# Three local changes and new step durations in a planner that orders a fused attention and expert kernel

## The chip, the core and the metric

The kernel runs on one core of a Trainium2 chip. The core has a matrix engine (PE, with its weight loads as PEld), a vector engine (DVE), an activation engine (ACT), a general engine (POOL) and a queue that issues transfers (SP). The metric is the device time of one execution in microseconds; lower is better. Matrix products write to PSUM, which has eight banks here, each of 128 x 512 float32.

## The reference, cut to what matters

```python
# stage 1: batch 4, 8 heads, 576 positions, 64 per head; heads 0-3 local (32 back), 4-7 strided (every 32nd)
scores = where(mask, q @ k.T / 8, -1e9); a = exp(scores - max)
attn = a / (a.sum(-1) + 1e-9) @ v
# stage 2: x (4, 576, 512)
h = relu(x @ w_in); u, v = h[..., :512], h[..., 512:]
v_n = (v - mean(v)) / sqrt(var(v) + 1e-6)
g = u * (w_spatial @ v_n + b_spatial);  x = g @ w_out
# stage 3: four experts, two of them chosen for each position by a gate
a_e = causal softmax((x wq_e) (x wk_e).T / 8), again with + 1e-9 in the divisor
out = sum over chosen e of weight_e * (a_e @ (x wv_e)) @ wo_e
```

All is float32; a product is made of three products of high and low parts.

## The kernel before, in words

Every piece of work is a *step* of a Python generator. A step says on which engine it runs (or on which of several), how long it is expected to take, what it waits for, and which buffers and PSUM banks it takes. A planner (`Plan.run`) plays the steps against these durations, takes on each engine the step that can start first (the lower rank among those that start within 0.05 us of it), and so fixes the order of the instructions on each engine. The chip runs each engine's list in that order, and semaphores keep the data right. A duration or a rank therefore changes no work, but the order, and with a choice of engines also the engine.

PSUM banks are shared out by kind: `d` for dense products (4), `s` for scores (2), `t` for transposes (2), `x` for values (3), eight of them at any time. `a1_scores` takes both `s` banks at once, `a1_values` two `x` banks.

Stage 1 for one pair of heads goes so: load q, k, v (SP); scores (PE, L497 or L507); mask and row maximum (DVE, L520 local, L555 strided); exponentials with row sums (ACT, L526, L561); `over_sums`, which adds 1e-9 to the sums (DVE, L534), inverts them (DVE, L535) and multiplies the rows (L537, DVE or POOL by the planner's choice); transposes (PE, L582) and values (PE, L640); high and low parts `xh`, `xl` (ACT and DVE, L652). There are four pairs per batch.

The first products with `w_in` need its words turned from float64 into float32 parts (`weight`: DVE L344 to L349). For the four blocks of the v half the sum of the two parts runs through PE (`summed`: L357 to L359 into an `s` bank, then a copy). The u half uses L371 (add) and L378 (low part) instead.

`v_half` makes the v half (PE, L289 to L291, 128 x 512), then `normalize`: statistics (DVE, L711 to L715), a power on POOL (`rstd`, L717), the scaling (DVE, L719), and the parts `vh` (ACT) and `vlo` (L699, mostly POOL). `u_half` is L289 to L291 with 128 x 288. `spatial` (PE, L794 to L799) needs all five v tiles of a batch. `late_constants` fills masks and zero tiles for stage 3 on POOL (L264 to L277): `mqk`, `mtail`, `bd`, `alone`, `tri`.

Where the planner sees PE without work in the first 46 us, it puts in products of zeros (`fill`, L217), one for each 0.4268 us that it expects to be free.

Of the kernel before, what the change touches and what calls it, by code (L numbers as in the profile page):

```python
# [7 lines left out]
F = dt.float32  # L8
R = dt.float32r
I32 = dt.int32  # L10
AF = mybir.ActivationFunctionType
# [142 lines left out]
def fused(tc, qk, vl, vs, win, wsb, woutT, wp, wo, out):  # L154
# [168 lines left out]
    def weight(keys, src, r0, rows, c0, cols, after=(), summed=False, alone=False):  # L323
# [10 lines left out]
        else:  # L334
# [6 lines left out]

            yield "dve", t_fast(2 * cols, 2) + t_dve(cols) + 0.25, (), dict(c=2)
            a, p2 = C([rows, cols], I32, "a"), C([rows, cols], I32, "p2")
# [7 lines left out]
            if summed:  # L351
                yield *hi_of(cols), (), dict(c=1)
                hi = C([rows, cols], R, "wh")
                copy(hi, f(a))
                yield "pe", t_mm(cols, 6), (), dict(s=1)
                ps = P([rows, cols], "s")
                pe.matmul(ps, ident, f(a), start=True, stop=False)  # L357
                pe.matmul(ps, unit, m, start=False, stop=False)
                pe.matmul(ps, minus, hi, start=False, stop=True)  # L359
                plan.give("c", 3)  # L360
                yield *out_of(cols), (), dict(c=1)
                wl = C([rows, cols], R, "wl")
                copy(wl, ps)
                plan.give("s")
                key, = keys
                W[key] = (hi, wl)
                plan.set(("W", key))
                return
# [111 lines left out]
    def a1_scores(b, hp):  # L480
# [4 lines left out]
        n = [len(a1_blocks(hp, g)) for g in range(2)]  # L485
        yield "pe", sum(n) * (0.1 if local else 0.09), [("qk", b, hp)], dict(s=2)
        st = A1[b, hp]
# [23 lines left out]
    def a1_local(b, hp, g):  # L511
        c0, c1 = LOCAL_GROUPS[g]
        n = c1 - c0
        yield "dve", t_dve(n * 64, n), [("mask", True), ("s1", b, hp)], dict(c=1)
        st = A1[b, hp]

        mx = sm([128, 8], "mx")
        a = C([128, n, 64], F, "a")
        for c in range(n):
            dve.tensor_tensor_reduce(a[:, c], st["ps"][g][:, c], mloc[:, min(c0 + c, 1)], op0=ALU.add, op1=ALU.min,  # L520
                                     scale=-0.125, scalar=3.0e38, accum_out=mx[:, c:c + 1])
        plan.give("s")
        yield "act", t_act(n * 64, n, 0.27), (), {}
        sums = sm([128, 8], "sums")
        for c in range(n):
            act.activation(a[:, c], a[:, c], AF.Exp, bias=mx[:, c:c + 1], scale=-1.0, accum_out=sums[:, c:c + 1])  # L526
        yield from over_sums(a, sums)
        st["a"][g] = a
        plan.set(("a", b, hp, g))

    def over_sums(x, sums):
        _, n, nk = x.shape
        yield "dve", 0.3, (), {}
        dve.scalar_tensor_tensor(sums[:, :n], sums[:, :n], 1e-9, sums[:, :n], op0=ALU.add, op1=ALU.max)  # L534
        dve.reciprocal(sums[:, :n], sums[:, :n])  # L535
        yield ("dve", "pool"), (t_dve(n * nk), t_pool(n * nk)), (), {}
        engine().tensor_mul(x, x, sums[:, :n].unsqueeze(2).broadcast_to([128, n, nk]))  # L537

    def a1_strided(b, hp, g):
# [17 lines left out]
        plan.give("s")  # L557
        yield "act", t_act(n * 54, n, 0.23), (), {}
        sums = sm([128, 8], "sums")
        for j, w in enumerate(width):  # L560
            act.activation(a[:, j, :w], a[:, j, :w], AF.Exp, bias=mx[:, j:j + 1], scale=-1.0,  # L561
                           accum_out=sums[:, j:j + 1])
        yield from over_sums(a[:, :n, :54], sums)
# [32 lines left out]
    def a1_values(b, hp):  # L596

        local = hp < 2
        yield ("pe", 18 * 0.05 if local else 11 * 0.07, [("v1", b, hp)] + [("aT", b, hp, g) for g in range(2)],
               dict(x=2))  # L600
# [41 lines left out]
        for g, part in enumerate(runs):  # L642
            cn = 64 * ((NL + 1 - g) // 2) if local else 54 * (4, 6)[g] + 36 * g
            yield *out_of(cn, len(part)), (), {} if g else dict(c=2)
            if g == 0:
                st["x"] = (C([128, S], R, "xh"), C([128, S], R, "xl"))
            xh, xl = st["x"]
            for cols, src in part:
                copy(cols(xh), src)
            yield "dve", t_dve(cn, len(part)), (), {}  # L650
            for cols, src in part:
                dve.tensor_sub(cols(xl), src, cols(f(xh)))  # L652
            if local:
                plan.give("x")
            elif g:
                plan.give("x", 2)
            plan.set(("x", b, hp, g))
# [46 lines left out]
    def normalize(ps, result):  # L704
# [12 lines left out]
        pool.tensor_tensor(rstd, rstd, neghalf, op=ALU.pow)  # L717
        yield "dve", t_fast(512, 1, 0.19), (), {}
        dve.tensor_scalar(vr, vr, mv[:, 0:1], rstd, op0=ALU.subtract, op1=ALU.mult)  # L719
# [386 lines left out]
    def a2_values(b, e):  # L1106
# [27 lines left out]
        copy(hi, px[:64])  # L1134
        yield "dve", t_dve(1024, 2), (), {}
        dve.tensor_sub(lo, px[:64], f(hi))
# [4 lines left out]
    def a2_tail_values(b, p):  # L1141
# [23 lines left out]
        for o in range(2):  # L1165
            copy(hi[o], px[:64, o, 0])
        yield "dve", t_dve(64, 6), (), {}
        for o in range(2):
# [51 lines left out]

    plan.add(90, late_constants())

# [135 lines left out]
```

## Time and profile before

| | us |
|---|---|
| median of three timed runs | 442.07 |
| the three runs | 441.53, 444.05, 442.07 |
| span of the profiled execution | 440.9 |
| PE busy in it | 424.2 |
| DVE busy | 312.2 |
| ACT busy | 282.2 |
| POOL busy | 140.0 |

The profiled execution shows its span and no other time; the median stands 1.2 us above that span. PE's clock was granted in full in every stretch up to the last one (1.00; 0.96 from 430 us on), the upper of its two levels, 2.4 GHz.

### The profile page before, as it was taken

Reading aid. Unit: us, or ns where it says so; the run is one execution under the profiler, and the core shown is the slowest. Engines: PE = TensorE matmul, PEld = TensorE weight load, DVE = VectorE, ACT = ScalarE, POOL = GpSimd, SP = SyncE. Lnnn points to the kernel's source line nnn. Section 1 sums busy time; section 2 is a strip of 40 time slices with the busy share of each in tenths; the row PEclk is TensorE's granted clock in tenths of the full one; section 3 lists DMA queues with packets and bytes.
Section 4 is the critical chain, followed back from the end, with each engine's and each line's share of the span. In section 5 each row is a group of like instructions: output and inputs, shape, how many; then the busy total and the mean of one; then the engine's idle time right before and its main releaser. Section 6 shows DMA issues by size and latency. Waiting matters only on the chain.

```text
span 440.9 us, 12067 instructions
## 1 busy us (share of the span) xinstructions
PE 424.2 (96%) x4424; PEld 382.0 (87%) x4429; DVE 312.2 (71%) x1155; ACT 282.2 (64%) x927; POOL 140.0 (32%) x237
## 2 busy tenths in 40 slices
PE   7798889999999999999999999999999999999996
PEld 4576679898999889998998899999999899988884
DVE  5879988545722783327998646789888998987861
ACT  4688598427930886205633533987787799769972
POOL 3317897422400371002675900021211111112300
PEclk9999999999999999999999999999999999999999
DMA  8998109200483005001000043711540415061234
GB/s 270 361 362 281 39 2 315 82 1 4 115 287 139 4 2 170 24 1 43 7 1 0 1 112 82 161 42 30 124 112 4 105 40 121 1 155 73 96 97 143
DMA packets 22814, 44.20 MB, mean 100 GB/s; under 512 B 3170, under 2 KB 5218, under 8 KB 22756
## 3 DMA queue, kind: packets, MB, share of 16 engines
q1 hardware_dynamic: 22756, 43.44, 33.2%
q8 instruction: 35, 0.57, 0.6%
q14 instruction: 23, 0.19, 0.1%
HBM read 27.18 MB, written 4.72 MB: 72 GB/s over the span
## 4 chain that ended last, share of the span: by engine, by line
PE 77%; DVE 11%; ACT 6%; POOL 2%; issue 2%; DVEq 0%; POOLq 0%; ACTq 0%
PE pd L289 14%; PE pd L291 14%; PE pd L290 14%; PE pd L794 4%; PE pd L795 4%; PE pd L796 4%; PE pt L1074 3%; PE px L640 3%; PE px L1120 2%; PE px L1122 2%; PE ps L497 2%; PE pt L582 2%; PE ps L990 2%; PE ps L989 2%; ACT a L1008 1%
## 5 line engine op out<-in xcount | busy, mean ns | idle before, releaser
L1001 ACT ACTIVATE a<-a,amx 128x128 f32<-128x128 f32 (+1 forms) x64 | 35.5, 556 | 6.7 <-DVE amx L977 6.3
L289 PE MATMUL pd<-xh,wh 128*128 128x288 f32 x128 | 39.0, 305 | 0.3 <-DVE mx L555 0.3
L289 PE MATMUL pd<-gh,fh 128*128 128x288 f32 x128 | 38.1, 298 | 0.0
L291 PE MATMUL pd<-gh,fl 128*128 128x288 f32 x128 | 37.9, 296 | 0.2 <-DVE fl L436 0.2
L794 PE MATMUL pd<-wh,vh 128*128 128x288 f32 x128 | 37.8, 295 | 0.0
L526 ACT ACTIVATE a<-a,mx 128x64 f32<-128x64 f32 x72 | 23.9, 334 | 21.5 <-DVE mx L520 21.5
L796 PE MATMUL pd<-wh,vlo 128*128 128x288 f32 x128 | 37.7, 294 | 0.0
L291 PE MATMUL pd<-xh,wl 128*128 128x288 f32 x128 | 37.7, 294 | 0.0
L290 PE MATMUL pd<-xl,wh 128*128 128x288 f32 x128 | 37.7, 294 | 0.0
L795 PE MATMUL pd<-wl,vh 128*128 128x288 f32 x128 | 37.7, 294 | 0.0
L290 PE MATMUL pd<-gl,fh 128*128 128x288 f32 x128 | 37.7, 294 | 0.0
L802 DVE TENSOR_TENSOR u<-pd,u 128x288 f32<-128x288 f32 x32 | 14.3, 453 | 31.7 <-PE pd L799 31.6
L977 DVE CUSTOM_DVE_ANT_0 a<-ps,mqk 128x128 f32<-128x128 f32 (+4 forms) x72 | 32.5, 481 | 4.3 <-PE ps L990 2.9
L537 POOL TENSOR_TENSOR a<-a,sums 128x320 f32<-128x320 f32 (+3 forms) x31 | 22.8, 736 | 38.1 <-DVE sums L535 17.4
L1008 ACT ACTIVATE a<-a,asums 128x384 f32<-128x384 f32 (+3 forms) x52 | 28.7, 566 | 6.6 <-DVE asums L1018 6.5
L561 ACT ACTIVATE a<-a,mx 128x54 f32<-128x54 f32 (+1 forms) x88 | 28.5, 335 | 3.2 <-DVE mx L555 3.2
L1010 POOL TENSOR_SCALAR a<-a,asums 128x256 f32<-128x256 f32 (+3 forms) x12 | 11.7, 977 | 59.1 <-DVE asums L1018 39.9
L1063 DVE TENSOR_TENSOR e<-pt,e 128x384 fp32r<-128x384 f32 (+1 forms) x48 | 27.5, 598 | 2.8 <-ACT e L310 2.3
L652 DVE TENSOR_TENSOR xl<-px,xh 128x108 fp32r<-128x108 f32 (+4 forms) x48 | 19.2, 433 | 14.4 <-ACT xh L310 14.4
L289 PE MATMUL pd<-wh,xh 128*128 128x512 f32 x64 | 26.5, 414 | 0.0
L316 ACT ACTIVATE vr<-pd 128x512 f32<-128x512 f32 x16 | 9.4, 593 | 25.8 <-PE pd L291 25.6
L1074 PE MATMUL pt<-ident,a 128*128 128x128 f32 x160 | 24.3, 275 | 1.0 <-ACT a L1008 1.0
(228 smaller groups left out, 1481.8 us busy)
## 6 DMA issues: line engine op xcount, KB each, us to landing
qk<-qk SPq DMA_DIRECT2D x64, 144.0 KB, 2.6
q<-in_qk_dram SPq DMA_DIRECT2D x16, 288.0 KB, 4.5
k<-in_qk_dram SPq DMA_DIRECT2D x16, 288.0 KB, 4.7
w<-in_win_dram SPq DMA_DIRECT2D x8, 512.0 KB, 6.1
v<-in_vl_dram SPq DMA_DIRECT2D x16, 256.0 KB, 5.4
out_dram<-o SPq DMA_DIRECT2D x16, 256.0 KB, 2.0
v<-in_vs_dram SPq DMA_DIRECT2D x8, 256.0 KB, 4.9
w<-in_woutT_dram SPq DMA_DIRECT2D x4, 512.0 KB, 6.3
```

The costliest lines, as they stand in the source:

```text
L289: pe.matmul(ps, ah, bh, start=i == 0, stop=False)
L290: pe.matmul(ps, ah, bl, start=False, stop=False)
L291: pe.matmul(ps, al, bh, start=False, stop=i == n - 1)
L561: act.activation(a[:, j, :w], a[:, j, :w], AF.Exp, bias=mx[:, j:j + 1], scale=-1.0, accum_out=sums[:, j:j + 1])
L794: pe.matmul(ps, vh[:, fs], wh[:, c0:c0 + cn], start=(i == 0), stop=False)
L795: pe.matmul(ps, vh[:, fs], wl[:, c0:c0 + cn], start=False, stop=False)
L796: pe.matmul(ps, vlo[:, fs], wh[:, c0:c0 + cn], start=False, stop=False)
L977: dve.tensor_tensor_reduce(a[:, s0:s0 + sn], ps, mask, op0=ALU.add, op1=ALU.min, scale=-0.125, scalar=m if s0 else 3.0e38, accum_out=m)
L1001: act.activation(a, a, AF.Exp, bias=m, scale=-1.0, accum_out=st["sums", e][:, i:i + 1])
L1008: act.activation(a, a, AF.Copy, scale=r)
L1063: dve.tensor_sub(el, ps, f(eh))
L1074: pe.transpose(ps[:, 128 * c:128 * c + 128], st["a", e, j][:, 128 * i:128 * i + 128], ident)
```

## The change

The sums of the weight words go to an `x` bank. Each softmax of stage 1 gets its sums from one of eight constant tiles of pairs whose second column holds 1e-9 (eight small fills on POOL at the start); a row sum over each pair replaces the addition, so the tile `rs` holds what `sums` held. The rank of `late_constants` goes from 90 to 350. Nine durations are replaced.

```diff
-            yield "dve", t_fast(2 * cols, 2) + t_dve(cols) + 0.25, (), dict(c=2)
+            yield "dve", 1.75, (), dict(c=2)
...
-                yield "pe", t_mm(cols, 6), (), dict(s=1)
-                ps = P([rows, cols], "s")
+                yield "pe", t_mm(cols, 6), (), dict(x=1)
+                ps = P([rows, cols], "x")
...
-                plan.give("s")
+                plan.give("x")
...
-        yield "pe", sum(n) * (0.1 if local else 0.09), [("qk", b, hp)], dict(s=2)
+        yield "pe", (1.15 if local else 0.95), [("qk", b, hp)], dict(s=2)
...
-        sums = sm([128, 8], "sums")
+        sums = next_sums()
...
+    EPS = [const.tile([128, 8, 2], F, name=f"eps{i}") for i in range(8)]
+    for t in EPS:
+        pool.memset(t, 1e-9)
...
+    def next_sums():
+        n_sums[0] += 1
+        return EPS[n_sums[0] % len(EPS)]
...
-        dve.scalar_tensor_tensor(sums[:, :n], sums[:, :n], 1e-9, sums[:, :n], op0=ALU.add, op1=ALU.max)
-        dve.reciprocal(sums[:, :n], sums[:, :n])
+        rs = sm([128, 8], "rs")
+        dve.tensor_reduce(rs[:, :n], sums[:, :n], op=ALU.add, axis=AX.X)
+        dve.reciprocal(rs[:, :n], rs[:, :n])
...
-            yield "dve", t_dve(cn, len(part)), (), {}
+            yield "dve", t_dve(cn, len(part), 0.15), (), {}
...
-        yield "dve", t_fast(512, 1, 0.19), (), {}
+        yield "dve", t_fast(512, 1, 0.3), (), {}
...
-        yield "dve", t_dve(1024, 2), (), {}
+        yield "dve", 1.4, (), {}
...
-        yield "dve", t_dve(64, 6), (), {}
+        yield "dve", 1.46, (), {}
...
-    plan.add(90, late_constants())
+    plan.add(350, late_constants())
```

The other two replaced durations are those of the strided exponentials (0.23 to 0.277 us each beside their elements) and of `a1_values` (1.25 and 0.9 us).

The orders differ almost from the start. Three places follow; in the rows after the change, lines from L534 on stand ten further down (L537 is L547, L717 is L727).

POOL before, around the masks for stage 3 (`a` are softmax rows, `m`, `wh`, `wl` weight parts):

```order
L371 TENSOR_TENSOR m_929<-m_929,a_843 128x512
L264 MEMSET mqk 128x640
L229 AFFINE_SELECT mqk<-mqk 128x128
L266 MEMSET mtail 128x288
L229 AFFINE_SELECT mtail<-mtail 64x64 x2
L378 TENSOR_TENSOR wl_1025<-m_929,wh_1021 128x512
L271 MEMSET bd_125 128x256
L537 TENSOR_TENSOR a_825<-a_825,sums_918 128x320
```

and POOL after the change, at the same place:

```order
L547 TENSOR_TENSOR a_782<-a_782,rs_918 128x320
L378 TENSOR_TENSOR wl_953<-m_839,wh_924 128x512
L555 MEMSET a_967 128x4x10
L555 MEMSET a_971 128x8x10
L557 MEMSET a_971 128x28
L558 MEMSET a_971 128x54
L371 TENSOR_TENSOR m_1005<-m_1005,a_945 128x512
L312 CAST wh_1041<-m_1005 128x512
L264 MEMSET mqk 128x640
```

The multiplication by the inverse sums of the first pair of batch 1 (`a_825` before, `a_782` now) no longer stands behind the masks. The two of the next local pair, which POOL had further on, are DVE's now (`a_911` here, and one more):

```order
L349 SCALAR_TENSOR_TENSOR m_1005<-w_604,p_946 128x512
L544 TENSOR_REDUCE rs_1009<-eps_135 128x4
L545 RECIPROCAL rs_1009<-rs_1009 128x4
L547 TENSOR_TENSOR a_911<-a_911,rs_1009 128x256
L565 ISA a_967,mx_1020<-ps_981,mstr 128x54
```

Up to the first `spatial` DVE has five such multiplications, before the change none.

POOL after the change, ahead of the first `vlo` (`st` are blocks of `w_spatial`):

```order
L378 TENSOR_TENSOR wl_1292<-st_1007,wh_1267 128x576
L378 TENSOR_TENSOR wl_1308<-m_1247,wh_1294 128x512
L378 TENSOR_TENSOR wl_1349<-st_1012,wh_1342 128x576
L378 TENSOR_TENSOR wl_1378<-st_1025,wh_1351 128x576
L396 MEMSET mb_1030 33x576
L547 TENSOR_TENSOR a_1203<-a_1203,rs_1403 128x7x54
L727 TENSOR_TENSOR rstd_1290<-rstd_1290,neghalf 128x1
L727 TENSOR_TENSOR rstd_1376<-rstd_1376,neghalf 128x1
L727 TENSOR_TENSOR rstd_1413<-rstd_1413,neghalf 128x1
L727 TENSOR_TENSOR rstd_1441<-rstd_1441,neghalf 128x1
L271 MEMSET bd_127 128x256
L275 MEMSET alone_128 64x512 x2
```

The four powers stand together; before, the first two had a multiplication behind each, and two `vlo` stood ahead of the last two. The `alone` fills, which stood ahead of all powers, now stand between them and the `vlo`.

PE before, ahead of the first `spatial` (rows 435 to 446 are a `v_half` of batch 1, those with `xt` the tail of v):

```order
L291 MATMUL pd_1568<-xh_912,wl_1193 128x288
L289 MATMUL pd_1591<-wh_309,xh_1158 128x512
L290 MATMUL pd_1591<-wl_375,xh_1158 128x512
...
L289 MATMUL pd_1618<-wh_309,xt_586 128x512
L290 MATMUL pd_1618<-wl_375,xt_586 128x512
...
L291 MATMUL pd_1618<-wh_689,xt_587 128x512
L794 MATMUL pd_1652<-wh_1208,vh_1442 128x288
```

and PE after the change:

```order
L291 MATMUL pd_1584<-wh_740,xt_577 128x512
L289 MATMUL pd_1599<-xh_466,wh_924 128x288
...
L290 MATMUL pd_1599<-xl_935,wh_1294 128x288
L291 MATMUL pd_1599<-xh_934,wl_1308 128x288
L804 MATMUL pd_1620<-wh_1267,vh_1473 128x288
```

The 12 matmuls of batch 1's `v_half` are gone from there (they come after the spatial steps). Over the whole of PE's list there are 33 products of zeros before the change and 25 after it; the first nine stand at the same place in both.

## Rows read from the trace of the kernel before

**Rows 1.** The page: span, and each engine's busy us, share and instructions.
```profile
span 440.9 us, 12067 instructions
PE 424.2 (96%) x4424; PEld 382.0 (87%) x4429; DVE 312.2 (71%) x1155; ACT 282.2 (64%) x927; POOL 140.0 (32%) x237
```

**Rows 2.** Busy us by stretch of 5 us: one stretch, and the sum to 80 us.
```profile
40.00:45.00 5.00, 3.88 (x55) 2.45 (x55) 4.82 (x28) 5.00 (x27) 4.40 (x11) 1.00 1.04 369
...
sum 80.00, PE 70.05 PEld 53.40 DVE 64.28 ACT 58.19 POOL 46.25; mean PE 4.38 PEld 3.34 DVE 4.02 ACT 3.64 POOL 2.89
```

**Rows 3.** The products of zeros on PE: as a group, and two pieces of the timeline.
```profile
L217 PE MATMUL pd<-zeros 128*128 128x512 bf16 x28 | 9.1, 460 | 1.7 <-DVE zeros L212 1.3 <-issue 0.3
...
1.25 4.02 PE L217 MATMUL pd<-zeros 128*128 128x512 bf16 x9 [1.25 <-DVE zeros L212]
...
32.74 0.81 PE L217 MATMUL pd<-zeros 128*128 128x512 bf16 x3
```

**Rows 4.** Timeline of PE (start, us): two transposes with their waits.
```profile
47.67 0.44 PE L582 MATMUL pt<-ident,a 128*128 128x128 f32 x2 [1.33 <-POOL a L537]
...
59.61 0.65 PE L582 MATMUL pt<-ident,a 128*118 128x128 f32 x4 [0.56 <-POOL a L537]
```

**Rows 5.** Timeline of POOL around the masks and zero tiles.
```profile
42.22 0.63 POOL L264 MEMSET mqk<- 128x640 f32 x1
...
44.72 1.51 POOL L378 TENSOR_TENSOR wl<-m,wh 128x512 fp32r<-128x512 f32 x1
...
46.44 1.18 POOL L537 TENSOR_TENSOR a<-a,sums 128x320 f32<-128x320 f32 x1
...
57.68 1.09 POOL L275 MEMSET alone<- 64x512 f32 x2
```

**Rows 6.** DVE: two pieces of the timeline, then groups by form.
```profile
44.99 1.26 DVE L534 SCALAR_TENSOR_TENSOR sums<-sums 128x4 f32<-128x4 f32 x1
...
46.38 0.66 DVE L349 SCALAR_TENSOR_TENSOR m<-w,p 128x512 f32<-128x512 uint32 x1
...
L534 DVE SCALAR_TENSOR_TENSOR sums<-sums 128x7 f32<-128x7 f32 x8 | 1.3, 165 | 1.3 <-ACT a L561 1.3
...
L902 DVE TENSOR_REDUCE gsum<-gex 128x5 f32<-128x20 f32 x4 | 0.7, 175 | 0.1
...
L537 DVE TENSOR_TENSOR a<-a,sums 128x256 f32<-128x256 f32 x1 | 0.4, 424 | 0.0
```

**Rows 7.** Timelines of DVE, POOL and PE: from the first statistics to the first spatial step.
```profile
55.47 0.15 DVE L715 TENSOR_SCALAR rstd<-mv 128x1 f32<-128x1 f32 x1
...
64.99 0.57 POOL L717 TENSOR_TENSOR rstd<-rstd,neghalf 128x1 f32<-128x1 f32 x1
...
72.96 1.51 DVE L719 TENSOR_SCALAR vr<-vr,mv,rstd 128x512 f32<-128x512 f32 x1
...
75.22 1.30 POOL L699 TENSOR_TENSOR vlo<-vr,vh 128x512 fp32r<-128x512 f32 x1 [1.03 <-ACT vh L310]
...
74.70 0.39 PE L289 MATMUL pd<-wh,xh 128*128 128x512 f32 x1
...
80.17 0.29 PE L794 MATMUL pd<-wh,vh 128*128 128x288 f32 x1
```

**Rows 8.** The weight sums: PE's first product of each, and ACT's copy of the result.
```profile
L357 PE MATMUL ps<-a,ident 128*128 128x512 f32 x8 | 4.2, 605 | 0.0
...
L310 ACT ACTIVATE wl<-ps x4: 582/586/598, 14.2 to 33.6; 128x512 fp32r<-128x512 f32 x4
```

**Rows 9.** Stage 3: busy us by stretch, their sum from 280 us, and one DVE step.
```profile
430.00:441.00 11.00, 6.53 (x30) 5.09 (x29) 1.31 (x6) 3.31 (x7) 0.00 (x0) 0.96 0.43 142
sum 161.00, PE 154.34 PEld 141.41 DVE 128.85 ACT 126.94 POOL 26.33; mean PE 10.29 PEld 9.43 DVE 8.59 ACT 8.46 POOL 1.76
...
L1137 DVE TENSOR_TENSOR cl<-cl,px x16: 689/690/694, 289.3 to 427.3; 64x512 fp32r<-64x512 f32 x16
```

**Rows 10.** A small fill on POOL, and POOL's first multiplication.
```profile
L253 POOL MEMSET neghalf<- x1: 88/88/88, 2.1 to 2.1; 128x1 f32 x1
...
9.99 0.87 POOL L537 TENSOR_TENSOR a<-a,sums 128x256 f32<-128x256 f32 x1 [6.00 <-DVE sums L535]
```

More of the change, by code (lines that the diff above doesn't have):

```diff
@@ L523, in a1_local @@
         yield "act", t_act(n * 64, n, 0.27), (), {}
-        sums = sm([128, 8], "sums")
+        sums = next_sums()
         for c in range(n):
-            act.activation(a[:, c], a[:, c], AF.Exp, bias=mx[:, c:c + 1], scale=-1.0, accum_out=sums[:, c:c + 1])
+            act.activation(a[:, c], a[:, c], AF.Exp, bias=mx[:, c:c + 1], scale=-1.0, accum_out=sums[:, c, :1])
         yield from over_sums(a, sums)
@@ L529, in a1_local @@
         plan.set(("a", b, hp, g))
+    EPS = [const.tile([128, 8, 2], F, name=f"eps{i}") for i in range(8)]
+    for t in EPS:
+        pool.memset(t, 1e-9)
+    n_sums = [0]
+    def next_sums():
+        n_sums[0] += 1
+        return EPS[n_sums[0] % len(EPS)]
     def over_sums(x, sums):
@@ L533, in over_sums @@
         yield "dve", 0.3, (), {}
-        dve.scalar_tensor_tensor(sums[:, :n], sums[:, :n], 1e-9, sums[:, :n], op0=ALU.add, op1=ALU.max)
-        dve.reciprocal(sums[:, :n], sums[:, :n])
+        rs = sm([128, 8], "rs")
+        dve.tensor_reduce(rs[:, :n], sums[:, :n], op=ALU.add, axis=AX.X)
+        dve.reciprocal(rs[:, :n], rs[:, :n])
         yield ("dve", "pool"), (t_dve(n * nk), t_pool(n * nk)), (), {}
-        engine().tensor_mul(x, x, sums[:, :n].unsqueeze(2).broadcast_to([128, n, nk]))
+        engine().tensor_mul(x, x, rs[:, :n].unsqueeze(2).broadcast_to([128, n, nk]))
     def a1_strided(b, hp, g):
@@ L557, in a1_strided @@
         plan.give("s")
-        yield "act", t_act(n * 54, n, 0.23), (), {}
-        sums = sm([128, 8], "sums")
+        yield "act", t_act(n * 54, n, 0.277), (), {}
+        sums = next_sums()
         for j, w in enumerate(width):
             act.activation(a[:, j, :w], a[:, j, :w], AF.Exp, bias=mx[:, j:j + 1], scale=-1.0,
-                           accum_out=sums[:, j:j + 1])
+                           accum_out=sums[:, j, :1])
         yield from over_sums(a[:, :n, :54], sums)
@@ L598, in a1_values @@
         local = hp < 2
-        yield ("pe", 18 * 0.05 if local else 11 * 0.07, [("v1", b, hp)] + [("aT", b, hp, g) for g in range(2)],
+        yield ("pe", 1.25 if local else 0.9, [("v1", b, hp)] + [("aT", b, hp, g) for g in range(2)],
                dict(x=2))
```

## The prediction, written before the run

> **What bounds the kernel now.** I read the page first: PE is busy for 424.2 of 440.9 us, no other engine for more than 312.2 [rows 1]. So the time is PE's work plus what PE loses, and only lost time can be won, since the change takes no product of the reference away. Then the table of stretches says where PE loses it. Up to 80 us it is busy for 70.05, so 9.95 us are idle [rows 2]. Part of the busy time is no work: the products of zeros take 9.1 us, of which the first nine take 4.02 while nothing has been loaded, which leaves 5.1 us [rows 3]. From 280 us on PE is busy for 154.34 of 161.0; the last stretch, where results are only copied and stored, has 4.5 of the 6.7 idle us, so 2.2 are lost in stage 3 [rows 9]. Between 80 and 280 us it hardly idles. That makes some 15 us to argue about in the opening (1.25 of them before the first product [rows 3]), two in stage 3, and a tail that the change doesn't touch.
>
> In the opening, the waits of PE lead to POOL and DVE. At 47.67 a transpose had waited 1.33 us for POOL's multiplication, at 59.61 another one 0.56 us [rows 4]. POOL began that first multiplication at 46.44 because the low part of a weight stood ahead of it from 44.72 for 1.51 us, and this one came behind the masks for stage 3, which begin at 42.22 [rows 5]. DVE is busy for 4.82 of 5 us in the same stretch and ACT for all of it, POOL for 4.40 [rows 2]: three engines are close to full, and what one is spared another may be given.
>
> **The masks and the multiplications.** In the new order the multiplication that PE waited for stands ahead of the masks, and the two of the next local pair are DVE's. On DVE one takes 0.42 us [rows 6], on POOL that one took 1.18 and stood behind 2.5 us of masks (42.22 to 44.72) [rows 5]. I take the wait of 1.33 us as gone: -1.3. Bounds: 0, if the wait goes to DVE, which is as full, and -1.9, if the 0.56 us goes too; there a fill of `alone` at 57.68 stood ahead [rows 5], and these fills are moved behind the powers. The moved masks still cost POOL the same, now ahead of a low part for the u half. That is hidden as long as `u_half` isn't PE's next work when it arrives; without that cover it costs the 2.5 us once.
>
> **Products of zeros.** There are 8 fewer (25 for 33), none of them among the first nine. Three in a row took 0.81 us, the first with its start-up, so 0.21 us each [rows 3]: 8 x 0.21 = 1.7. They are a sign of gaps more than a cost: the planner puts them where it sees no work, and now it has transposes, values and `v_half` parts there. I take -1.7. Bounds: 0, if the new work waits for data exactly as long; -3.4, if idle time of the same size that stood beside the zeros goes with them.
>
> **The row sum.** 32 instructions for 32. The addition takes 0.165 us undisturbed (7 columns), the nearest row sum 0.175, over 20 elements [rows 6]: 32 x 0.01 = 0.3 us of DVE spread over four batches, hidden where PE has dense work. But the addition of 44.99 took 1.26 us [rows 6]. It ended at 46.25, just as POOL's subtraction ended (44.72 + 1.51 = 46.23) [rows 5]: an instruction that reads two tiles waited while POOL read its own. A row sum reads one. I still take 0. What comes behind the inverse is L349 at 46.38 [rows 6], which also reads two tiles and would have stood there in its place, and the sums' user is POOL itself, which was not free before 46.2. Bounds: +0.3, and -2.0, if DVE keeps the 1.1 us in two such places.
>
> The Trainium skill (SBUF — State Buffer, Who interferes with whom) says the same in general: a DVE instruction with two inputs in SBUF contends with a POOL instruction that reads SBUF, and a row sum on trn2 never does. The trace of 44.99 agrees with its first half [rows 6]; no run here shows the second. By the rule alone each stretched addition would be a gain, as in the third rival.
>
> **Small fills.** Eight constant tiles at 0.09 us make 0.7 us on POOL, which then stood idle for 6.0 us before its first multiplication at 9.99 [rows 10]. Cost 0; without that idle time, 0.7.
>
> **Weight sums in `x`.** Before the change PE did not wait at all ahead of the sums [rows 8], so the bank kind cost nothing there; what it changes is that scores, which need both `s` banks, can go earlier, and values, which need two `x` banks, can be held by a sum until ACT has copied it. I take 0. Bounds: the gain is inside the zeros above; the loss is one copy, 0.59 us [rows 8], twice.
>
> **The first spatial block.** Here the new order takes something away. `v_half` of batch 1 and the tail of v, twelve products each, stood ahead of it from 74.70 to 80.17 [rows 7], so 2.7 us each. The last `vlo` ended at 75.22 + 1.30 = 76.52 [rows 7]: 3.65 us of slack. With the `v_half` gone 0.9 is left, and if PE comes 3.0 us earlier, v must be ready some 2.1 us earlier. It can be a little earlier: the first power was ready to go at 55.62 and POOL took it at 64.99 [rows 7], since it stood behind fills and low parts; the `alone` fills (three pairs of 1.09 us [rows 5]) no longer stand there, but one more addition, two casts and one more low part do. DVE's work up to the fourth scaling is nearly the same: five multiplications more (5 x 0.42 = 2.1 [rows 6]), fewer subtractions and small copies. So I expect v about 1.3 us earlier and PE to wait the rest: +0.8. Bounds: 0 and +3.6 (v not earlier, and one pair of `alone` fills, now among the `vlo`, behind it all). The displaced `v_half` is done later at the same price.
>
> **Stage 3.** Two DVE steps get longer estimates: L1137 and its twin make about 1.4 us, as the trace has it (2 x 0.69 [rows 9]) where 1.2 was planned, and the six small ones of the tail had been planned at 0.5. The planner hands a few copies from ACT to DVE and three scalings from ACT to POOL. PE loses 2.2 us there; I take a fifth of it, -0.5, with 2.2 in either direction.
>
> **Sum**: -1.3 - 1.7 + 0 + 0 + 0.8 - 0.5 = -2.7 us. The profiled span becomes 440.9 - 2.7 = 438.2, the median 442.07 - 2.7 = 439.4, 0.6% less. What a measurement of this kernel can tell from no change is about 0.5%, 2.2 us. The forecast's own range is 437.5 to 441.2.
>
> **Rivals.**
>
> *The gain stays inside the opening* (0.22). DVE, ACT and POOL hold nearly the same work, DVE is 96% busy at 40 to 45 us [rows 2], and so the first spatial block begins when v is ready, whatever PE did ahead of it. Then only the 0.9 us of slack and some of stage 3 are won, or nothing: 442.07 - 0.5 = 441.6. For it: the full engines. Against it: DVE's time is full of stretched instructions, as at 44.99 and 72.96 (1.51 us for a scaling [rows 7]), and POOL has fewer reads to stretch them with.
>
> *v is late, slower* (0.14). The place is POOL's list ahead of the first `vlo`: four low parts, a fill, a multiplication, four powers and the `alone` fills stand in a row. At 1.51, 0.57, 0.81 (estimate from 1.18 for a stretched one), 0.57 and 1.09 us that is 6.0 + 0.6 + 0.8 + 2.3 + 1.1 = 10.8 us, and three `vlo` with a second pair of fills behind it, 3 x 1.30 + 1.09 = 5.0. If the casts that the low parts need come no sooner than 66 us, v is ready at 66 + 15.8 = 81.8. PE arrives at 80.17 - 2.7 - 3.0 = 74.5 and waits 7 us, less 1.2 for the products that need no last `vlo`. 442.07 - 3.5 + 5.8 = 444.4. It decides from 64 us on. For it: POOL did take the first power only at 64.99. Against it: the casts of the `w_spatial` blocks are on DVE and ACT ahead of the statistics, and POOL has been spared three multiplications.
>
> *POOL and DVE stop blocking each other* (0.20). With the row sum never held up and five multiplications off POOL, DVE keeps 2 x 1.1 us in the opening and the scalings shrink from 1.51 towards their short form; v is ready 3 us earlier, PE's +0.8 goes and its other waits for DVE with it: 442.07 - 2.7 - 0.8 - 2.0 = 436.6. This is where the rule of the skill's page on SBUF would lead. For it: the stretched rows. Against it: the neighbours of the row sum read two tiles.
>
> **How the numbers follow.** Forecast 0.44, of which 0.28 lies below 439.9 and 0.16 within 0.5%; first rival 0.22 (0.20 same, 0.02 slower); second 0.14, slower; third 0.20, faster. Faster 0.28 + 0.20 = 0.48, same 0.36, slower 0.16. The predicted time is the forecast's, 439.4. The range takes the first rival whole, the third down to 435.3 and of the second what lies below 443.2; a tenth on either side is left out.
>
> **What would show it.** The masks: no wait for POOL's multiplication above 0.6 us at 40 to 60 us. The zeros: some 25 products, and PE's idle time to 80 us near 8 us. The row sum: 32 at about 0.17 us, none stretched, with L349 stretched instead. The spatial block: its first product at about 75 us, behind a wait of up to a microsecond for `vlo` or `vh`. Stage 3: idle within 1 us of before. The prediction is wrong if PE's first spatial product comes before 73 us (the third rival), if PE waits for v for over 3 us (the second), or if stage 3 alone moves by more than 2 us.

## The result: slower by 0.65%

The changed kernel takes 445.18 us (median of 14 runs, 444.41 to 449.59), the kernel before 443.44 beside it (14 runs): a ratio of 1.0065, 95% interval 1.0045 to 1.0085. The forecast was 439.4 us, a ratio of 0.994, with a range up to 443.2; the result lies outside it. Two executions of sums_in_s below, at 451 us, ran in a slower state and are left out of its row.

The page of the changed kernel (its profiled execution took 444.76 us) has a span of 442.7 us, 1.8 more than in [rows 1], the same busy time of PE, and a row of TensorE's granted clock that is no longer full everywhere (40 slices of 11 us, in tenths):

```profile
span 442.7 us, 12084 instructions
...
PE   7897988999999999999999999999999999999975
...
PEclk9998899999999999999999999999999999999989
```

**The opening.** Windows of 1 us on PE (start and end, length, busy us, granted clock, DMA share, GB/s):

```profile
39.00:40.00 1.00, 0.10 (x6) 1.00 1.02 366
...
41.00:42.00 1.00, 0.34 (x2) 0.91 1.01 221
42.00:43.00 1.00, 0.40 (x2) 0.50 0.70 161
43.00:44.00 1.00, 1.00 (x17) 0.50 0.39 102
...
47.00:48.00 1.00, 1.00 (x4) 0.50 0.00 0
48.00:49.00 1.00, 1.00 (x4) 0.67 0.00 0
49.00:50.00 1.00, 1.00 (x6) 1.00 0.03 8
```

PE was nearly idle at 39 and again from 41 to 43 us. From 42 to 48.6 us the clock stood at 0.50, the lower level (1.2 GHz); from 43 us on PE was busy all the time, at half its rate. Counted over these windows (lost share of the clock times busy us), that is some 3 us of PE's work. The timelines of PE, DVE and POOL (start, us) say what PE waited for at 42 us, and what the half clock did:

```profile
42.60 0.66 PE L592 MATMUL pt<-ident,a 128*128 128x128 f32 x2 [1.27 <-DVE mx L565]
43.06 0.63 PE L217 MATMUL pd<-zeros 128*128 128x512 bf16 x1
43.62 2.35 PE L650 MATMUL px<-aT,v 64*64 64x32 f32 x72
...
40.61 1.31 DVE L547 TENSOR_TENSOR a<-a,rs 128x256 f32<-128x256 f32 x1
...
42.38 0.08 DVE L565 DVE_READ_ACCUMULATOR2_ANT mx<- 128x1 f32 x1
...
40.38 1.27 POOL L371 TENSOR_TENSOR m<-m,a 128x512 f32<-128x512 f32 x1 [1.76 <-DVE rs L544]
```

The transposes need the rows that DVE multiplies at 40.61, and a bank of PSUM. The multiplication took 1.31 us where I had 0.42 [rows 6]; it ended at 41.92, just behind POOL's addition (40.38 + 1.27 = 41.65), which reads two tiles as it does. It isn't what PE waits for last: the row names L565, the masks of the next scores, and in the kernel's list the transposes take the very bank from which these four masks read. The fourth ended at 42.46, and PE went on 0.14 us behind it, 0.68 behind the multiplication. But the masks stand behind the multiplication on DVE, so its length counts all the same. So the wait of [rows 4] for POOL is gone; the list of waits (us in total, times, longest) has at most 0.7 us left for POOL, and a wait for DVE, by the transposes of the next pair, in its place:

```profile
PE pt L1099 <- ACT a L1018: 2.7, 1, 2.7
PE px L650 <- issue: 1.5, 2, 1.1
PE pt L592 <- DVE mx L565: 1.3, 1, 1.3
...
PE pt L592 <- POOL a L547: 0.7, 1, 0.7
```

Up to 80 us PE is idle for 9.7 us (9.95 before). The first spatial product stands at 77.59 without a wait, for 80.17 in [rows 7]; twelve products of `v_half`, 2.7 us, had moved behind it. v was no bound: POOL's last low part ended at 70.64 + 2.54 = 73.18. PE's last wait ahead of that block was one of 1.17 us for ACT's copy of the tail, `xt`.

```profile
75.66 0.50 PE L291 MATMUL pd<-wh,xt 128*128 128x512 f32 x1 [1.17 <-ACT xt L310]
...
77.59 0.29 PE L804 MATMUL pd<-wh,vh 128*128 128x288 f32 x1
...
70.64 2.54 POOL L709 TENSOR_TENSOR vlo<-vr,vh 128x512 fp32r<-128x512 f32 x2
```

The first score of stage 3 is a good milestone for all that came ahead of it. It stands at 272.34 in the trace of before and at 271.85 after, so between these two executions 0.5 us is won up to there:

```profile
272.34 0.23 PE L989 MATMUL ps<-qk,qk 128*128 128x128 f32 x1
...
271.85 0.23 PE L999 MATMUL ps<-qk,qk 128*128 128x128 f32 x1
```

**Stage 3.** From that score to the last product before took 436.14 - 272.34 = 163.8 us; now 437.95 - 271.85 = 166.1. PE's timeline of the end, first two rows of before, then after the change:

```profile
413.67 0.29 PE L1033 MATMUL ps<-qk,bd 128*128 128x288 f32 x1
...
436.14 0.39 PE L291 MATMUL pd<-wh,ct 128*128 128x512 f32 x1
...
422.47 0.30 PE L1043 MATMUL ps<-qk,bd 128*128 128x288 f32 x1
...
423.60 0.27 PE L1132 MATMUL px<-e,v 128*128 128x128 f32 x1
426.56 0.66 PE L1099 MATMUL pt<-ident,a 128*128 128x128 f32 x4 [2.70 <-ACT a L1018]
427.06 1.24 PE L1084 MATMUL pt<-ident,a 128*128 128x128 f32 x7
428.00 1.97 PE L1162 MATMUL px<-te,v 128*128 128x128 f32 x8
...
434.42 0.50 PE L291 MATMUL pd<-wh,cl 128*128 128x512 f32 x1 [0.71 <-DVE cl L1147]
...
437.95 0.39 PE L291 MATMUL pd<-wh,ct 128*128 128x512 f32 x1
```

PE stands still for 2.70 us, and then runs at the lower level: eight products of the last tail take 1.97 us, and the clock is 0.50 at 428 to 430 us:

```profile
425.00:426.00 1.00, 0.00 (x0) 1.00 0.00 0
...
428.00:429.00 1.00, 1.00 (x7) 0.50 0.00 0
429.00:430.00 1.00, 1.00 (x7) 0.50 0.00 0
```

Nothing of the projections (`project`, L289 to L291 with `ch`) lies between 423.5 and 433 us. Before, five groups of three stood from 426.1 to 431 us, PE was busy throughout, and the clock stayed at 1.00:

```profile
420.00:430.00 10.00, 10.00 (x62) 8.45 (x62) 6.32 (x13) 6.94 (x15) 0.00 (x0) 1.00 0.35 108
```

The chain of the last tail begins with its last scores (L1033, now L1043) and goes by DVE and ACT to the transposes. Before, these scores stand 22.5 us ahead of the last product, and PE has other work for the 11.8 us from them to the transposes, 27 products of the projections among it. Now they stand 15.5 us ahead of it, the chain takes 3.8 us, and PE has 1.1 us of other work for it, 3 products of the projections among it; the others have gone ahead of the scores.

So there are two theories to test: the opening's gain is eaten by DVE's multiplication and the half clock behind PE's gap; and stage 3 loses some 2 us through the two durations 1.4 and 1.46 alone. Rivals: the row sum, the bank, or the rank costs the time; or the end is the scatter of one execution.

### The profile page after: what moved, and what is told of

It reads as the page before. It is cut to its first block, busy times and chain, and to the rows that moved or that the text cites. A ratio compares the mean times of both kernels' runs of the same rounds, so it can differ in the third digit from the quotient of the medians.

```text
span 442.7 us, 12084 instructions
## 1 busy us (share of the span) xinstructions
PE 424.2 (96%) x4421; PEld 384.2 (87%) x4421; DVE 318.6 (72%) x1159; ACT 282.7 (64%) x925; POOL 139.3 (31%) x243
## 4 chain that ended last, share of the span: by engine, by line
PE 84%; DVE 8%; ACT 4%; issue 2%; DMA 1%; POOL 0%; ACTq 0%; DVEq 0%; POOLq 0%
PE pd L289 15%; PE pd L291 15%; PE pd L290 14%; PE pd L804 4%; PE pd L805 4%; PE pd L806 4%; PE pt L1084 4%; PE px L650 3%; PE ps L1000 2%; PE pt L592 2%; PE ps L999 2%; PE px L1132 2%; PE px L1162 2%; PE px L1130 2%; PE ps L497 2%
## 5 line engine op out<-in xcount | busy, mean ns | idle before, releaser
L1020 POOL TENSOR_SCALAR a<-a,asums 128x128 f32<-128x128 f32 (+3 forms) x15 | 12.5, 837 | 99.0 <-DVE asums L1028 38.1
L289 PE MATMUL pd<-xh,wh 128*128 128x288 f32 x128 | 38.5, 301 | 0.0
L289 PE MATMUL pd<-gh,fh 128*128 128x288 f32 x128 | 38.0, 297 | 0.0
L291 PE MATMUL pd<-xh,wl 128*128 128x288 f32 x128 | 37.7, 295 | 0.0
L291 PE MATMUL pd<-gh,fl 128*128 128x288 f32 x128 | 37.7, 295 | 0.0
L547 POOL TENSOR_TENSOR a<-a,rs 128x320 f32<-128x320 f32 (+3 forms) x26 | 19.4, 746 | 44.3 <-DVE rs L545 15.4
L1018 ACT ACTIVATE a<-a,asums 128x512 f32<-128x512 f32 (+3 forms) x49 | 27.5, 582 | 3.5 <-DVE asums L1028 3.5
L289 PE MATMUL pd<-wh,xh 128*128 128x512 f32 x64 | 27.2, 425 | 0.0
L310 ACT ACTIVATE e<-pt 128x384 fp32r<-128x384 f32 (+1 forms) x48 | 23.7, 520 | 5.1 <-PE pt L1084 4.4
L291 PE MATMUL pd<-wh,xl 128*128 128x512 f32 x64 | 25.5, 399 | 0.0
```

The lines of the kernel that those rows point to most:

```text
L289: pe.matmul(ps, ah, bh, start=i == 0, stop=False)
L291: pe.matmul(ps, al, bh, start=False, stop=i == n - 1)
L1018: act.activation(a, a, AF.Copy, scale=r)
```

## The experiments

All were timed beside the kernel before. The last two columns are from the one profiled execution of each; the clock is the median over its timed executions. Undone means the two durations of stage 3 put back. The kernels were timed in several rounds, so between rows of different rounds the ratios compare better than the microseconds.

| kernel | us, median | ratio to before, 95% | clock | first score, us | score to last product |
|---|---|---|---|---|---|
| changed kernel | 445.18 | 1.0045 to 1.0085 | 0.986 | 271.85 | 166.10 |
| rowsum_alone | 442.85 | 0.9978 to 1.0025 | 0.992 | 272.01 | 164.10 |
| stage3_durations_alone | 445.16 | 1.0012 to 1.0063 | 0.992 | 273.74 | 168.08 |
| stage3_durations_undone | 443.31 | 0.9979 to 1.0042 | 0.990 | 273.35 | 163.83 |
| denser_zeros | 447.40 | 1.0058 to 1.0132 | 0.988 | 272.81 | 166.27 |
| gap_zeros (undone) | 442.17 | 0.9980 to 1.0017 | 0.997 | 271.65 | 163.84 |
| multiplications_on_pool (undone) | 441.74 | 0.9957 to 0.9987 | 0.992 | 271.94 | 163.91 |
| tail_zeros | 444.57 | 1.0023 to 1.0053 | 0.992 | 276.55 | 164.96 |
| gap_zeros_before | 444.14 | 0.9999 to 1.0034 | 0.996 | 274.57 | 163.89 |
| pool_and_zeros (undone) | 440.38 | 0.9915 to 0.9957 | 0.999 | 269.85 | 163.89 |
| sums_in_s (undone) | 444.90 | 1.0009 to 1.0055 | 0.992 | 274.72 | 163.83 |
| bank_alone | 446.00 | 1.0044 to 1.0094 | 0.987 | 276.97 | 163.79 |
| rank_undone (undone) | 443.45 | 0.9985 to 1.0032 | 0.992 | 272.03 | 163.79 |
| only_1_46 | 441.42 | 0.9929 to 0.9982 | 0.992 | 272.15 | 162.26 |
| only_1_40 | 441.14 | 0.9929 to 0.9977 | 0.991 | 271.32 | 161.91 |
| pool_zeros_1_40 | 438.20 | 0.9859 to 0.9909 | 0.999 | 269.62 | 161.94 |

The kernel before had medians of 443.0 to 443.7 us and a clock of 0.995 to 0.996 in these rounds: its first profile, with the clock reduced only at the very end, was one of its better executions. The six replaced durations of the opening weren't tried alone.

**rowsum_alone**: in the kernel before, the row sum alone; every instruction keeps its place.

```diff
-        dve.scalar_tensor_tensor(sums[:, :n], sums[:, :n], 1e-9, sums[:, :n], op0=ALU.add, op1=ALU.max)
+        dve.tensor_reduce(rs[:, :n], sums[:, :n], op=ALU.add, axis=AX.X)
...
-        sums = sm([128, 8], "sums")
+        sums = next_sums()
```

> The kernel before with the row sum over pairs alone: every step keeps its place on every engine, so only durations can move. My theory (the row sum costs nothing; the loss is in two stretches of the order) expects the kernel before's time within 0.3 us, the 32 row sums at 0.15 to 0.17 us, and the addition's stretched place (1.26 us at 44.99) gone while a neighbour that reads two tiles is stretched in its place by about 1 us. The rival, that the row sum or its constant tiles cost the time, expects 1 to 3 us more than the kernel before. A second rival, that the row sum is a gain that the new order hides, expects 1 to 2 us less.

The ratio is 1.0001: the row sum and its eight fills cost nothing that can be told from it. DVE's and POOL's timelines, at the place of [rows 6]:

```profile
44.99 0.15 DVE L544 TENSOR_REDUCE rs<-eps 128x4 f32<-128x8 f32 x1
...
45.27 1.47 DVE L349 SCALAR_TENSOR_TENSOR m<-w,p 128x512 f32<-128x512 uint32 x1
...
44.72 1.47 POOL L378 TENSOR_TENSOR wl<-m,wh 128x512 fp32r<-128x512 f32 x1
```

The addition took 1.26 us here and L349 0.66; now the row sum takes 0.15 and L349 1.47, under the same instruction of POOL. What comes next on DVE starts at 46.67 for 46.96: 0.3 us remain of the 1.1. The stretch falls on the next instruction with two tiles. The Trainium skill (SBUF — State Buffer, Who interferes with whom) says that a DVE instruction with two inputs in SBUF contends with a POOL instruction that reads SBUF, and that a row sum on trn2 never does. Here the trace agrees with both halves: 1.47 us for L349, 0.15 for the row sum.

**stage3_durations_alone** (in the kernel before) and **stage3_durations_undone** (in the changed one), two of the eight steps that get new durations (not nine, as said at the change):

```diff
-        yield "dve", t_dve(1024, 2), (), {}
+        yield "dve", 1.4, (), {}
...
-        yield "dve", t_dve(64, 6), (), {}
+        yield "dve", 1.46, (), {}
```

> The kernel before with the durations 1.4 and 1.46 alone: the order is that of before up to stage 3 and that of after from there. My theory (these two numbers use up the projections too early, so that the last chain of the tail stands uncovered, and the products behind it run at half the granted clock) expects a PE stall of 2.5 to 3 us ahead of four transposes near 424 us, a granted clock near 0.5 for some 4 us behind it, and 1.5 to 2.5 us more than the kernel before. The rival, that the loss is all in the opening and the difference in the last 20 us is the scatter of one execution, expects the kernel before's time within 0.5 us.

> The changed kernel with the two stage 3 durations put back: the opening is that of after, the last 30 us that of before. My theory expects 1.8 us less than the changed kernel, so within 1 us of the kernel before (ratio 0.999 to 1.003), with PE busy all through 416 to 436 us and the clock at 1.00 there; the half clock near 42 to 49 us stays. The rival (all of the loss lies in the opening) expects 2 to 3 us more than the kernel before, as in the changed kernel.

Both came as expected: with the two durations alone the kernel before takes 1.95 us more (445.16 for 443.21), and without them the changed kernel takes 1.87 less (443.31 for 445.18). The stall is there in the one (2.68 us) and gone in the other. The length of stage 3 is the cleanest sign: 163.8 to 164.1 us in the ten traces with the old pair of durations, 166.1 and more with the new pair, unless zeros stand in the stall. The place of the last tail's scores goes with it: 15.5 to 17.5 us ahead of the last product in the three traces with the new pair and no zeros in the stall, 22.5 to 22.6 in the ten.

**tail_zeros**: the changed kernel, and in the stall

```diff
+        if (b, p, n) == (B - 1, 1, 0):
+            for _ in range(24):
+                pe.matmul(ps, zeros[:, :128], zeros[:, :w], start=True, stop=True)
```

> The changed kernel with 24 products of zeros (256 columns, some 0.1 us each) ahead of the first transposes of the last tail, in the stall of 2.70 us. They add no work to a busy engine. If half of the loss of stage 3 is the half clock behind the stall (products from 427 to 431 us at half rate, about 2 us of PE's time, part of it hidden behind the chain), the clock stays near 1.00 there and the time falls by 0.5 to 1.5 us from the changed kernel's 445.2. If the uncovered chain alone sets the end, the clock stays up too and the time stays within 0.4 us. If the clock falls in the stall whatever is in it, both stay as they are.

The median is 444.57, 0.6 us less, with intervals that overlap; in the profile the clock is at 1.00 from 420 to 437 us, and stage 3 is 1.1 us shorter (164.96):

```profile
420.00:437.00 17.00, 16.55 (x113) 1.00 0.09 32
```

So in these two executions about half of the 2.3 us was the stall itself, and half the half clock behind it.

**only_1_46** and **only_1_40**: the changed kernel with one of the two durations put back. The order of PE then has twelve products of the projections ahead of the last tail's values (only_1_46), or 30 in all for the end (only_1_40; the changed kernel 18, before 24). In both, the last tail's scores are back at 21 and 23 us ahead of the last product, with 27 and 30 products of the projections between them and the transposes.

> The changed kernel with the duration 1.4 put back and 1.46 kept. The order then keeps twelve products of the last projections ahead of the last tail's values and 18 behind them. My theory (the loss of stage 3 is the uncovered chain, which only both durations together make) expects no stall of over 1 us from 416 to 436 us and 443.3 within 0.8 us. The rival (the loss comes with the longer duration of the six small steps itself, by what it moves between the engines) expects 445.2 within 0.5 us.

> The changed kernel with 1.46 put back and 1.4 kept. The order keeps 30 products of the projections for the end, six more than the kernel before. My theory expects no stall of over 1 us in the last 30 us ahead of the projections and 443.3 within 0.8 us. The rival (the longer duration of L1137's step itself is the loss) expects 445.2 within 0.5 us; a second rival, that the chain is covered less because six products more stand behind it, expects a stall of 0.5 to 1.5 us ahead of the last tail's values, and 444 to 445.

Neither stalls, so neither duration costs by itself. My number was wrong too: they are 1.9 and 2.2 us faster than stage3_durations_undone (2.5 by the ratios), not equal to it, and stage 3 is 1.5 to 1.9 us shorter than before. PE's time from the first score to the end, without and with 1.4 (length, busy us):

```profile
273.35:437.60 164.25, 162.00 (x1138) 1.00 0.35 88
```

```profile
271.32:433.65 162.33, 160.93 (x1138) 1.00 0.36 89
```

0.85 us less idle, and 1.07 less busy time for the same 1,138 products. Why these pack more tightly stays open.

**denser_zeros**: the changed kernel with twice the zeros in all of the first 46 us.

```diff
-        for _ in range(int(us / (0.4268))):
+        for _ in range(int(us / (0.2134))):
```

> The changed kernel with a product of zeros for each 0.2134 us that the planner expects to be free in the first 46 us instead of each 0.4268: 55 zeros for 25, nothing else moves. My theory (PE was nearly idle from 38.6 to 43.5 us, and the granted clock then fell to half from 42 to 48.6 us, which cost about 3 us of PE's time) expects the clock at 1.00 from 40 to 50 us, the 72 value products at 1.36 us for 2.35, and the changed kernel's time less 1.5 to 3 us, so from 0.5 us below to 1 us above the kernel before. The rival, that the first spatial product waits for v or that the new order idles there whatever the clock, expects the changed kernel's time within 0.7 us, the 3 us coming back as waits up to 77 us. A third way: the added zeros stand in front of work that was ready, and the time grows by up to 2 us.

A miss: 447.40; the interval leaves out the gain that I expected, though it overlaps with that of the changed kernel. The clock held at 40 to 50 us, but the zeros stood ahead of loaded work at the start:

```profile
1.25 5.49 PE L217 MATMUL pd<-zeros 128*128 128x512 bf16 x18 [1.25 <-DVE zeros L212]
6.67 1.21 PE L497 MATMUL ps<-k,q 64*32 64x64 f32 x72
```

The first scores came 1.9 us later than in the changed kernel (4.78). At the first score of stage 3 this execution is 1.0 us behind the changed kernel's (272.81 for 271.85). And the clock fell later, from 59 to 62 us, behind another gap. Zeros in every place that the planner takes for free are no gain.

**gap_zeros**: stage3_durations_undone, with more zeros only in the three gaps near 40 us.

```diff
-        for _ in range(int(us / (0.4268))):
+        for _ in range(int(us / (0.4268 if plan.t["pe"] < 36 else 0.1067))):
```

> The changed kernel with the two stage 3 durations put back, and with four times as many products of zeros as planned in the three gaps from 36 us on of the planner's time alone (19 for 4; the first 21 stay). They stand ahead of the transposes that wait for DVE's multiplication. My theory (the new order saves about 2 us of PE's work and idle time ahead of the first spatial product, and pays them back at half clock after the gap at 38.6 to 45 us) expects no half clock from 40 to 60 us in most executions, a mean granted clock of about 0.994 for the 0.990 without the zeros, and 1 to 2 us less than without them (443.31), so 441.3 to 442.3, 0.2 to 0.4% under the kernel before. The rival (the clock's fall is not bound to this gap, and comes later where it doesn't come here) expects the same mean clock and 443.3 within 0.5 us. A third way: the zeros stand ahead of ready work and cost up to 1 us.

The clock's median rose from 0.990 to 0.997, more than expected, and the median time fell by 1.1 us to 442.17. The interval of the ratio still holds 1.000, so of the time this is only an indication. In the profiled execution the clock held from 40 to 50 us and fell at 57.5 to 61 instead, around waits of 0.30 and 0.83 us, as the rival has it. So the zeros make a fall rarer; they don't rule it out.

**gap_zeros_before**: the same line in the kernel before.

> The kernel before with four times as many zeros in the gaps from 36 us on of the planner's time (its 6 become about 28). The control for gap_zeros: the kernel before has half clock in the opening in some executions too (its mean granted clock runs from 0.988 to 1.000, its time from 441.3 to 446.4). My theory expects its fall at 43 to 50 us to become rarer, the clock's median to rise from 0.996 to 0.998, and 0 to 1 us less, less than what gap_zeros gains. The rival, that zeros there stand in front of ready work, expects 0.5 to 2 us more.

444.14, with the clock as it was. That fits the rival, that the zeros (15 from 41.95 on, 9 from 45.41) delay ready work, but the interval just reaches 1.000, and the profiled execution has its half clock at 23 to 26 us, ahead of every added zero. No gain is shown; the loss is only indicated.

**multiplications_on_pool**: stage3_durations_undone, and

```diff
-        yield ("dve", "pool"), (t_dve(n * nk), t_pool(n * nk)), (), {}
+        yield "pool", t_pool(n * nk), (), {}
```

> The changed kernel with the two stage 3 durations put back, and every multiplication by the inverse sums on POOL. Six were DVE's, at 1.35 us where I had taken 0.42, and PE waited 1.27 (2.81 in another execution) for one of them near 42 us. My theory (DVE's choice moves the wait from POOL to DVE, no more) expects no transposes that wait for DVE's multiplication, another wait of 1 to 2 us for POOL's instead, and a time within 1 us of 443.3. The rival, that DVE's multiplications alone undo the gain, expects the wait to go without another in its place, and 1.5 to 2.5 us less, 441 to 442. A second rival: POOL becomes late for the low parts of v, the first spatial product stands at 81 us or later for 77.6 to 79.1, and the time grows by 2 us or more.

441.74, an interval wholly below 1: the first rival, DVE's multiplications undo the gain, comes nearest, 1.6 us. The wait near 42 us is down to 0.25 us. Yet the rival's account is wrong in that a worse one took its place: 5.37 us for POOL, and half clock behind it (PE's timeline; all engines from 50 to 60 us: busy us of PE, PEld, DVE, ACT, POOL, then the clock):

```profile
54.05 0.68 PE L592 MATMUL pt<-ident,a 128*118 128x128 f32 x2 [5.37 <-POOL a L547]
...
50.00:60.00 10.00, 5.95 (x42) 4.67 (x46) 9.83 (x40) 7.19 (x31) 8.49 (x8) 0.66 0.01 2
```

**pool_and_zeros**: the same with zeros in this wait.

```diff
+            if (b, hp, g, i0) == (1, 2, 0, 0):
+                for _ in range(44):
+                    pe.matmul(pt.rearrange("p a b -> p (a b)"), zeros[:, :rows], zeros[:, :128 * (k + last)], start=True, stop=True)
```

> multiplications_on_pool (441.74) with 44 products of zeros (256 columns, some 0.1 us each, 4.7 us together) ahead of the transposes that waited 5.37 us for POOL there; behind that wait the products ran at half the granted clock from 54 to 58 us. My theory (a wait of PE in the opening costs twice: itself, where nothing else bounds, and some 2 us of half clock behind it) expects the clock at 1.00 from 50 to 60 us, a median clock of 0.996 for 0.992, and 0.8 to 1.6 us less, so 440.1 to 440.9. The rival (v is not ready earlier, so PE only waits later) expects the same time within 0.4 us, with a wait ahead of the first spatial product at 77.7 us. A third way: the zeros hold up the transposes, 0.5 to 1 us more.

```profile
47.63 5.01 PE L593 MATMUL pt<-zeros 128*118 128x256 bf16 x44
53.08 0.43 PE L595 MATMUL pt<-ident,a 128*118 128x128 f32 x2 [0.44 <-POOL a L547]
...
50.00:60.00 10.00, 9.14 (x101) 7.78 (x98) 9.76 (x42) 7.99 (x33) 8.25 (x9) 1.00 0.01 2
```

As expected: 440.38, 1.36 us less (1.6 by the ratios), the clock's median at 0.999. Nothing but the 44 zeros was added. The transposes still wait for POOL until 53.08, but the work behind them runs at full rate. Against the kernel before this opening wins 0.64%, some 2.8 us: a gain of the size that I had forecast for it is there once the waits for DVE and the half clock are gone.

**sums_in_s**, **bank_alone**, **rank_undone**: one part of the change each, in the changed kernel with the durations undone, or in the kernel before.

```diff
-                yield "pe", t_mm(cols, 6), (), dict(x=1)
+                yield "pe", t_mm(cols, 6), (), dict(s=1)
...
-    plan.add(350, late_constants())
+    plan.add(90, late_constants())
```

> The changed kernel with the two stage 3 durations put back and the sums of weight words in an s bank again: what is left of the change is the row sum, the rank 350 and the opening's durations. The planner then puts in 34 zeros (before 33, changed 25). My theory (the bank is what gives the opening its new order, and that order wins in work what it loses in clock) expects 443.3 within 0.7 us and a median clock nearer to the kernel before's (0.995) than to 0.990. The rival that the x bank itself costs the time (values held by a sum) expects 1 to 2 us less, the rival that it is what gains expects 1 to 2 us more.

> The kernel before with the sums of weight words in an x bank alone: 27 zeros for 33, stage 3 as before. My theory expects fewer zeros and an order as in the changed kernel's opening, a median clock below the kernel before's (0.995) by about 0.004, and a time within 0.8 us of it. The rival that the x bank costs expects 1 to 2 us more at the same clock; the rival that it gains 1 to 2 us less.

> The changed kernel with the two stage 3 durations and the rank 90 put back: PE's order hardly moves, the masks for stage 3 stand ahead again on POOL. My theory (the rank moves POOL's fills, and the wait that it removes comes back as one for DVE) expects 443.3 within 0.6 us, and a wait of PE for DVE's multiplication near 42 us as in the changed kernel. The rival, that the rank gives the 1.3 us that I forecast, expects 444.4 to 444.9 and a wait for POOL's multiplication of over 1 us at 44 to 50 us.

The rank shows no effect on the time: 443.45 for 443.31, with a wait of 1.85 us for DVE near 43 us as in the changed kernel. A wait of 2.54 us for POOL's multiplication is there too, at 56.92 and not where the rival had it. The bank missed both expectations: put back, the median is 1.6 us higher (444.90 for 443.31; the intervals overlap, so this isn't shown), and alone in the kernel before it costs 2.3 (446.00 for 443.72). Both ways the median rises, so the bank seems to have no price of its own; each combination is another order. In bank_alone the clock is at 0.51 from 52 to 62 us, around waits of 1.08 and 1.75 us, and falls again behind one of 2.61 us for DVE's multiplication that ends at 68.28.

**pool_zeros_1_40**: pool_and_zeros with the duration 1.4.

> pool_and_zeros (440.38) with the duration 1.4 kept: the order of only_1_40 in stage 3 on the opening that runs at full clock. Both theories of stage 3 must hold here too: mine expects 440.4 within 0.6 us, the rivals 441.1 to 442.3. That the clock in the opening stays up is tested a second time: a median clock of 0.997 or more.

438.20, a ratio of 0.9884: the gain of stage 3 (2.2 us) adds to that of the opening. My expectation, 440.4, had missed that gain as in only_1_40; the clock's median is 0.999, as expected. This version beats both kernels.

## Why the prediction was wrong, point by point

I forecast 2.7 us less; beside the kernel before, 1.7 us more was measured. Stage 3 and the opening make about half of the miss each (2.4 and 2.3 us, by the medians of another round). (The forecast also started from 442.07, a median of three; the kernel before takes 443.44.)

**Stage 3 (-0.5, with 2.2 either way): the step that failed, +1.9.** I took "a fifth" of PE's idle time as a gain, from which engine gets a few copies. What decides is where the projections stand to the last tail's scores, since they cover the chain that begins there. The new order puts these scores 15.5 us ahead of the end, for 22.5 before, and leaves 3 projections between them and the transposes, for 27; the order of the changed kernel shows it before any run, and I hadn't looked there. (That 18 projections stand behind the chain, for 24, is not it: only_1_46 has 18 too and doesn't stall.) The stall of 2.7 us and the half clock share the loss about equally in the two profiles. Single durations gain instead, so this was no cost of a duration but an order that fell out badly.

**Masks and multiplications (-1.3): failed by its bound 0.** "I take the wait of 1.33 us as gone": a wait for DVE took its place, 1.27 us in the changed kernel and 2.81 in stage3_durations_undone. In the changed kernel 0.6 us of it lie under DVE's multiplication, which took 1.31 us and not the 0.42 of a row that no work of POOL disturbs (all six took 0.82 to 1.53, at 216 to 378 columns), and 0.5 under the four masks behind it, whose bank the transposes need; my term had neither that length nor the masks. The rank, to which I put this term, shows no effect (rank_undone).

**Zeros (-1.7): the count was right (25), its worth was not.** I wrote that they are a sign of gaps more than a cost. The gap at 38.6 to 43 us stayed, emptier, and some 3 us of PE's work were lost in the half clock behind it. The prediction has no term for the clock, because the one profile of before had it at 1.00 up to the end. Together the opening came to +0.1 in the median (443.31 for 443.21) where -2.2 was forecast.

**Row sum and fills (0): right, in all its parts.** 32 row sums, none over 0.17 us, L349 stretched instead, ratio 1.0001. Third rival refuted: the neighbours read two tiles.

**The bank (0):** within the change no loss shows, but my bounds (two copies of 0.59 us) fail for bank_alone, +2.3, where another order and its half clock come in.

**First spatial block (+0.8): failed.** It came at 77.59, not about 75, and behind no wait of its own. v was ready 3.3 us earlier than before, where I had 1.3, so it bounds nothing; PE was late by its half clock and its own waits, the last of them 1.17 us for `xt`. (My upper bound, +3.6, is 2.1 + 1.1 = 3.2 by its own terms.) The second rival (v late) is refuted. The first rival, that the opening gains nothing, gave the right size for the opening by the wrong mechanism.

## What to carry to other kernels

Where a planner's numbers change, read the new order at the end of the program first: where does the last chain of dependent steps begin, and does independent work still stand behind its first product? Price a wait of the matrix engine twice, once for itself and once for the rate of what comes behind it; zeros in that very wait were worth 1.4 us here, zeros in every supposed gap nothing, and perhaps a loss of 2. A better estimate of one step's duration is no gain by itself: each of two corrections gave some 2 us, and both together lost 2.

## What the runs showed of the hardware that was not expected

The granted clock falls to its lower level for some 3.4 to 10 us behind some gaps of PE (0.51 from 429.5 to 439.8 us in the tail of stage3_durations_alone). In the changed kernel PE had stood idle for 0.97 and 1.27 us around the fall of the opening, and for 2.70 us ahead of that of the tail. It doesn't fall behind the same ones in each execution: before and rowsum_alone have the same order, and from 44 to 50 us one ran at 1.00 and the other at 0.50 (busy us of PE, PEld, DVE, ACT, POOL, then the clock; before first):

```profile
44.00:50.00 6.00, 4.67 (x52) 3.39 (x50) 5.78 (x8) 3.98 (x16) 5.92 (x7) 1.00 0.30 74
...
44.00:50.00 6.00, 5.99 (x43) 4.87 (x43) 5.79 (x9) 2.65 (x12) 5.68 (x7) 0.50 0.27 67
```

In stage3_durations_undone the twelve timed executions go from 441.67 us at a mean clock of 0.996 to 446.94 at 0.983, some 4 us for each 0.01. A fall need not cost time: that one of rowsum_alone shows no loss by the first score (272.01 us, for 272.34). The rows above suggest why: DVE is busy for 5.8 of the 6 us in both, and at full clock PE stands idle for 1.3 of them, which the half clock fills. That DVE sets the pace there isn't shown. Zeros kept the clock up in the last tail (1.00 from 420 to 437 us) and in the wait of 5.4 us, so the work ahead need not be real work.
